# Moving the filter's loads, its folding and its spectrum into the first batch of an attention and long-convolution kernel

## Chip, cores, metric

One core of one Trainium2 chip. The metric is the device time of one execution in microseconds (us), lower is better; a kernel's figure is the median of its runs.

## The reference

Random-feature attention on 8 batches of 8 heads, 576 positions, 64 values per head, then a gated long convolution along the positions:

```python
phi(x)  = concat(cos(x @ omega.T), sin(x @ omega.T)) / sqrt(m)     # m = 128 features
kv      = einsum('bhsm,bhsd->bhmd', phi(k), v);  z = phi(k).sum(axis=2)
attn    = (phi(q) @ kv) / (phi(q) . z)                             # [8, 8, 576, 64] -> x [8, 576, 512]
x1, x2, x3 = split(x @ w_proj, 3)                                  # w_proj [512, 1536]
conv    = irfft(rfft(x2, axis=1) * rfft(filter_fft, axis=0))       # filter_fft [576, 512]
out     = (x1 * conv * x3) @ w_out
```

The FFT is done as matrix products with a cosine/sine basis (`fwd`), over sums and differences of each row with its partner half a period away (the "fold"). The filter needs this once, each batch once.

## The kernel before

A batch goes through four "pairs" (two heads each). The attention of batch b+1 runs between the convolution steps of batch b. Batches 0 and 1 get their k and q transposed by TensorE (`tk`, `tkt`, `tq`), later ones by DMA. The filter was handled like this:

```python
def run(self):
    self.first_loads()                 # k, q, v of batch 0
    self.front(0, 0)                   # features of the first pair
    self.second_loads()                # k, q of batch 1: into yg0, yg1, w
    self.v_loads(1)
    self.weights()                     # basis fwd, filter (into tc0, tc1, yT), w_proj
    for b in range(B + 1):
        for hp in range(4):
            if b < B: self.pair(b, hp)
            if b == hp == 1:
                self.fold_filter()     # six tensor_tensor on VectorE
                self.filter_spectrum() # 17 matmuls, ten copies by ScalarE
            if b: self.hyena(b - 1, hp)      # part 1 is spectrum(b - 1): yp, tc, yg
# ... (cut)
def fold_filter(self):
    with self.tc.issue_after(self.marks["strip", 1, 0].ins):
        for c in range(NC):
            for p, odd, _, n in _filter_rows(c):
                nc.vector.tensor_tensor(ff[c][p:p+n], f[p:p+n, 0], f[p:p+n, 1], SUB if odd else ADD)
# ... (cut)
def k_features(self, b, hp):
    if b < 2: self.first_k(b, hp)      # tk: transpose by TensorE; evacuated by VectorE (b = 0) or ScalarE (b = 1)
    # thk = matmul -> angles by VectorE -> shifted angles by GpSimd -> sine by ScalarE (kf)
# ... (cut)
def spectrum(self, b):                 # of a batch
    for g in range(2):
        # yp = matmuls; tc0, tc1 = yp * filter spectrum (VectorE); yg = tc0 + tc1 (GpSimd)
```

## Time and profile before

| | before |
|---|---|
| median of runs | 424.49 us (423.31 to 424.59, 3 runs; 424.3 beside the changed kernel, with a fourth) |
| span of the profiled run | 419.9 us |
| TensorE, VectorE, ScalarE, GpSimd busy | 80%, 70%, 57%, 53% |
| TensorE's first transposes of batch 1 (`tkt`) | 36.46 us |
| last transposes of batch 0's attention, `tx` | 48.74 us |
| first `tx` of batch 1 | 69.06 us |
| batch 0's spectrum `yp` on TensorE | 79.30 us |

The busy shares are means over very different stages; the marks in the lower half of the table tell more, because each is a point that TensorE, which works in program order, must pass. What fills the SyncE queue early (start, time of issue, what; x is the count):

```profile
11.61 0.64 SPq L319 DMA_DIRECT2D ka<-in_k_dram  x1
...
17.29 8.93 SPq L325 DMA_DIRECT2D qa<-in_q_dram  x2
...
30.96 1.11 SPq L169 DMA_DIRECT2D fwd<-fwdc  x1
32.19 18.52 SPq L200 DMA_DIRECT2D f<-in_moe_filter_fft_dram  x12
```

Batch 1's k and q are issued from 10 to 26 us; only then come the basis (`fwd`) and, to about 50.7 us, the filter `f`. The filter is not needed until 70 us.

### The profile page before, as it was taken

Reading aid. Unit: us, or ns where it says so; the run is one execution under the profiler, and the core shown is the slowest. Engines: PE = TensorE matmul, PEld = TensorE weight load, DVE = VectorE, ACT = ScalarE, POOL = GpSimd, SP = SyncE. Lnnn points to the kernel's source line nnn. Section 1 sums busy time; section 2 is a strip of 40 time slices with the busy share of each in tenths; the row PEclk is TensorE's granted clock in tenths of the full one; section 3 lists DMA queues with packets and bytes.
Section 4 is the critical chain, followed back from the end, with each engine's and each line's share of the span. In section 5 each row is a group of like instructions: output and inputs, shape, how many; then the busy total and the mean of one; then the engine's idle time right before and its main releaser. Section 6 shows DMA issues by size and latency. Waiting matters only on the chain.

```text
span 419.9 us, 9053 instructions
## 1 busy us (share of the span) xinstructions
PE 337.1 (80%) x3714; PEld 225.8 (54%) x3714; DVE 293.4 (70%) x527; ACT 239.8 (57%) x318; POOL 222.1 (53%) x199
## 2 busy tenths in 40 slices
PE   3777666996798977896989889897989788988982
PEld 2565534374455754565556655575556644673650
DVE  3777746679857888497849885788759883862640
ACT  1676764556686458833784488545784478223322
POOL 0546632178653947385836865494726483523350
PEclk9859699799699999999899989996999999999998
DMA  6999999007951592149523873259210012002103
GB/s 175 289 283 270 234 235 156 2 4 152 142 158 32 102 201 82 39 108 156 127 65 101 104 135 114 74 85 172 88 27 0 2 52 64 2 2 70 42 2 113
DMA packets 71465, 44.76 MB, mean 107 GB/s; under 512 B 38656, under 2 KB 64896, under 8 KB 71424
## 3 DMA queue, kind: packets, MB, share of 16 engines
q1 hardware_dynamic: 53712, 34.12, 31.9%
q0 software_dynamic: 17712, 10.06, 17.7%
q8 instruction: 29, 0.48, 0.4%
q14 instruction: 12, 0.10, 0.1%
HBM read 36.83 MB, written 16.52 MB: 127 GB/s over the span
## 4 chain that ended last, share of the span: by engine, by line
PE 36%; DVE 28%; ACT 12%; POOL 11%; issue 8%; DMA 3%; SPq 1%; POOLq 0%; DVEq 0%; ACTq 0%
PE xg L112 10%; DVE tc L557 7%; PE kv L493 6%; PE op L112 5%; ACT qf L477 5%; PE xc L112 4%; DVE angk L418 4%; POOL yT L596 3%; POOL angq L419 3%; DVE angq L418 3%; ACT kf L456 3%; PE nd L510 3%; POOL vl L400 2%; DVE xsd L516 2%; DMA out_dram<-o 2%
## 5 line engine op out<-in xcount | busy, mean ns | idle before, releaser
L477 ACT ACTIVATE qf<-angq 128x1728 f16<-128x1728 int16 (+1 forms) x48 | 70.4, 1480 | 42.6 <-PE nd L510 22.4
L456 ACT ACTIVATE kf<-angk 128x2048 f16<-128x2048 int16 x32 | 61.1, 1909 | 42.0 <-POOL angk L419 31.5
L112 PE MATMUL xg<-xT,wp 128*128 128x288 f16 x512 | 72.0, 286 | 1.1 <-ACT w L574 0.3
L419 POOL TENSOR_SCALAR angk<-angk 128x1024 int32<-128x1024 int32 x32 | 33.5, 1048 | 63.5 <-DVE angk L418 63.1
L418 DVE TENSOR_SCALAR angq<-thq 128x864 int32<-128x864 f32 (+1 forms) x48 | 45.8, 954 | 24.4 <-ACT qf L477 20.0
L112 PEld LDWEIGHTS <-wp 128*128 128x128 f16 x512 | 48.5, 97 | 20.6 <-issue 4.1
L400 POOL TENSOR_TENSOR vl<-vf,vh 128x512 f16<-128x512 f32 x32 | 39.0, 1219 | 28.8 <-ACT vh L399 28.4
L558 POOL TENSOR_TENSOR yg<-tc,tc 128x1024 fp32r<-128x1024 f32 x16 | 37.4, 2358 | 31.5 <-DVE tc L557 30.4
L596 POOL TENSOR_TENSOR yT<-w,cv 128x576 f16<-128x576 f32 x32 | 45.5, 1436 | 15.3 <-DVE cv L595 8.1
L576 DVE TENSOR_TENSOR w<-xg,w 128x288 f32<-128x288 f32 x64 | 27.4, 453 | 37.1 <-ACT w L574 19.6
L419 POOL TENSOR_SCALAR angq<-angq 128x864 int32<-128x864 int32 (+1 forms) x48 | 43.0, 896 | 16.5 <-DVE angq L418 16.1
L493 PEld LDWEIGHTS <-kf 128*128 128x128 f16 x1024 | 43.7, 100 | 13.2 <-issue 11.1
L112 PE MATMUL op<-wo,yT 128*128 128x512 f16 (+1 forms) x160 | 41.4, 390 | 6.0 <-POOL yT L596 6.0
L574 ACT ACTIVATE w<-xg 128x288 f32<-128x288 f32 x64 | 24.6, 407 | 37.7 <-PE xg L112 37.0
L418 DVE TENSOR_SCALAR angk<-thk 128x1024 int32<-128x1024 f32 x32 | 39.0, 1219 | 9.0 <-ACT qf L477 4.4
L510 PE MATMUL nd<-kvz,qf 128*128 128x65 f16 x640 | 27.5, 198 | 20.5 <-DVE kvz L498 19.1
L493 PE MATMUL kv<-vh,kf 128*128 128x65 f16 x512 | 38.5, 198 | 6.1 <-ACT w L574 5.6
L112 PE MATMUL x2p<-wp,eo 128*128 128x512 f16 x160 | 36.3, 379 | 4.9 <-ACT x L546 2.9
L510 PEld LDWEIGHTS <-qf 128*128 128x128 f16 x640 | 25.1, 100 | 26.3 <-issue 23.8
L493 PE MATMUL kv<-vl,kf 128*128 128x64 f16 x512 | 37.3, 197 | 0.8 <-POOL vl L400 0.8
L112 PE MATMUL xc<-inv,yg 128*128 128x288 f32 x128 | 33.4, 352 | 0.1
L609 ACT ACTIVATE o<-op 128x512 f32<-128x512 f32 (+1 forms) x40 | 22.8, 592 | 15.2 <-PE op L112 10.0
(86 smaller groups left out, 628.8 us busy)
## 6 DMA issues: line engine op xcount, KB each, us to landing
vf<-in_v_dram SPq DMA_DIRECT2D x7, 1024.0 KB, 5.3
qD<-in_q_dram POOLq DMA_DIRECT2D x6, 576.0 KB, 7.0
kD<-in_k_dram POOLq DMA_DIRECT2D x6, 512.0 KB, 5.9
ka<-in_k_dram SPq DMA_DIRECT2D x4, 512.0 KB, 10.5
out_dram<-o SPq DMA_DIRECT2D x8, 256.0 KB, 2.6
out_dram<-o SPq DMA_DIRECT2D x8, 224.0 KB
wp<-in_moe_w_proj_dram POOLq DMA_DIRECT2D x1, 1536.0 KB, 16.1
out_dram<-o SPq DMA_DIRECT2D x8, 192.0 KB
```

Source lines behind the costliest of these rows:

```text
L112: nc.tensor.matmul(outap, l, r, start=(i == 0), stop=(i == n - 1))
L400: nc.gpsimd.tensor_tensor(self.vl[hp], vp, vh, ALU.subtract)
L418: self.nc.vector.tensor_scalar(into, th, TO_PHASE, None, ALU.mult)
L419: self.pool_mark = self.nc.gpsimd.tensor_scalar(t[:, 1], t[:, 0], 1.0, TURN / 4, ALU.mult, ALU.add)
L456: self.marks["k", b, hp] = nc.scalar.activation(kf.rearrange("p t r a c m -> p t (r a c m)"), ang, AF.Sin, scale=TO_ANGLE)
L477: nc.scalar.activation(self.qf[b][:, :, a0 : a0 + n].rearrange("p t a r i -> p t (a r i)"), ang, AF.Sin, scale=TO_ANGLE)
L493: nc.tensor.matmul(ps[:, hh, t, : 1 + D] if i < 5 else ps[:, hh, t, :D], l, r_, start=(i == 0), stop=(i == len(terms) - 1),)
L510: nc.tensor.matmul(ps[:, c], qfh[:, t, SOFF[c] : SOFF[c] + 128], kvz[:, hh, t], start=(t == 0), stop=(t == 1),)
L557: nc.vector.tensor_tensor(t[i], ps[:, None, :].broadcast_to([128, 2, DM]), hc, ALU.mult)
L558: nc.gpsimd.tensor_tensor(self.yg[g], t[0], t[1], ALU.add)
L576: nc.vector.tensor_tensor(w[:, ns], ps, w[:, ns], ALU.mult)
L596: nc.gpsimd.tensor_tensor(self.yT[b][:, dc], self.w.pop((b, dc)).rearrange("p a s -> p (a s)"), cv.rearrange("p c z i -> p (c z i)"), ALU. ...
```

## The change

The intent: the filter's fold and spectrum stand in series for nine microseconds, once per run, so do them earlier, where engines idle. The basis and the filter are loaded directly behind batch 0, in front of batch 1; GpSimd folds; the spectrum and the first transposes of batch 1 go between the pairs of batch 0.

```diff
 def run(self):
         self.front(0, 0)
-        self.second_loads()
-        self.v_loads(1)
         self.weights()
+        self.second_loads()              # v of batch 1 now inside, behind the first k and q blocks
@@
-                if b == hp == 1:
-                    self.fold_filter()
-                    self.filter_spectrum()
+                if b == 0:
+                    self.opening(hp)
+    def opening(self, hp):
+        if hp == 1:
+            self.fold_filter()
+            self.first_k_tails(1)
+            self.first_k(1, 0)
+        elif hp == 2:
+            self.filter_spectrum(0)
+            self.first_k(1, 1)
+        elif hp == 3:
+            self.filter_spectrum(1)
+            self.filter_spectrum(2)
@@ fold_filter: no issue_after any more
-                    nc.vector.tensor_tensor(...)
+                nc.gpsimd.tensor_tensor(...)
@@ buffers of the loads
-        f{c}: tc0, tc1, tc1, tc0, yT                 ka1: yg0, yg1      qa1: w (4 tiles)
+        f0, f1, f4: yg0, yg1, yT; f2, f3 as halves in w (17 DMAs, 12 before)
+        ka1: tc0 (2 tiles)   qa1: tc1 (2 tiles)
@@ filter_spectrum: hre, him become one tile h; one copy fewer per group
... (cut)
```

More of the change, by code (lines that the diff above doesn't have):

```diff
@@ L39 @@
 QW = 4 * S
-FTAG = [("tc0", 2), ("tc1", 2), ("tc1", 2), ("tc0", 2), ("yT", 1)]
 QGROUPS = [(0, 3, 3), (6, 3, 3), (12, 2, 2)]
@@ L194, in filter_loads @@
         every4 = self.filt.rearrange("(z i r) d -> r i z d", z=2, r=4)
+        whole = {0: ("yg0", 1), 1: ("yg1", 1), 4: ("yT", 1)}
         self.fl = []
         for c in range(NC):
-            f = mo.tile([128, 2, DM], FP32, name=f"f{c}", tag=FTAG[c][0], bufs=FTAG[c][1])
+            if c in whole:
+                tag, bufs = whole[c]
+                f = mo.tile([128, 2, DM], FP32, name=f"f{c}", tag=tag, bufs=bufs)
+                parts = [(f, slice(0, 2))]
+                self.fl.append([f[:, 0], f[:, 1]])
+            else:
+                halves = [mo.tile([128, 1, DM], FP32, name=f"f{c}_{z}", tag="w", bufs=4) for z in range(2)]
+                parts = [(f, slice(z, z + 1)) for z, f in enumerate(halves)]
+                self.fl.append([f[:, 0] for f in halves])
             for p, _, lo, n in _filter_rows(c):
                 for blk, i, m, at in _pieces(lo, n, EB):
-                    nc.sync.dma_start(f[p + at : p + at + m], every4[BLOCKS[blk], i : i + m])
-            self.fl.append(f)
+                    for f, z in parts:
+                        nc.sync.dma_start(f[p + at : p + at + m], every4[BLOCKS[blk], i : i + m, z])
     def fold_filter(self):
@@ L207, in fold_filter @@
         self.ff = ff = [ffs[c // 2][:, c % 2] for c in range(NC)]
-        with self.tc.issue_after(self.marks["strip", 1, 0].ins):
-            nc.vector.memset(ff[2], 0.0)
-            for c in range(NC):
-                f = self.fl[c]
-                for p, odd, _, n in _filter_rows(c):
-                    nc.vector.tensor_tensor(
-                        ff[c][p : p + n], f[p : p + n, 0], f[p : p + n, 1], ALU.subtract if odd else ALU.add
-                    )
-    def filter_spectrum(self):
-        nc, cst, fwd, ff = self.nc, self.cst, self.fwd, self.ff
-        self.hre = [cst.tile([128, 2, DM], FP16, name=f"hre{g}", tag=f"hre{g}") for g in range(2)]
-        self.him = [cst.tile([128, 2, DM], FP16, name=f"him{g}", tag=f"him{g}") for g in range(2)]
-        self.hmix = cst.tile([128, DM], FP16, name="hmix", tag="hmix")
-        hre, him = self.hre, self.him
-        for g in range(2):
-            ps = self.bank([128, DM], f"hps{g}")
-            _mm_acc(nc, ps, [(fwd[:, 2 * g, c], ff[c]) for c in GRP[2 * g]])
-            nc.scalar.copy(hre[g][:, 0], ps)
-            nc.scalar.copy(him[g][:, 1], ps)
-            ps = self.bank([128, DM], f"hpi{g}")
-            _mm_acc(nc, ps, [(fwd[:, 2 * g + 1, c], ff[c]) for c in GRP[2 * g + 1]])
-            nc.scalar.copy(hre[g][:, 1], ps)
-            nc.scalar.mul(him[g][:, 0], ps, -1.0)
-            if g == 0:
-                nc.scalar.copy(him[0][:1, 1], ps[:1])
-                nc.vector.memset(hre[0][:1, 1], 0.0)
-                nc.vector.memset(him[0][:1, 0], 0.0)
-        ps = self.bank([128, DM], "hpm")
-        _mm_acc(nc, ps, [(fwd[:, 5, c], ff[c]) for c in GRP[5]])
-        nc.scalar.copy(self.hmix, ps)
@@ new lines, in fold_filter, with filter_spectrum @@
+        nc.gpsimd.memset(ff[2], 0.0)
+        for c in range(NC):
+            f = self.fl[c]
+            for p, odd, _, n in _filter_rows(c):
+                nc.gpsimd.tensor_tensor(
+                    ff[c][p : p + n], f[0][p : p + n], f[1][p : p + n], ALU.subtract if odd else ALU.add
+                )
+    def filter_spectrum(self, g):
+        nc, cst, fwd, ff = self.nc, self.cst, self.fwd, self.ff
+        if g == 2:
+            self.hmix = cst.tile([128, DM], FP16, name="hmix", tag="hmix")
+            ps = self.bank([128, DM], "hpm")
+            _mm_acc(nc, ps, [(fwd[:, 5, c], ff[c]) for c in GRP[5]])
+            nc.scalar.copy(self.hmix, ps)
+            return
+        h = self.h[g] = cst.tile([128, 4, DM], FP16, name=f"h{g}", tag=f"h{g}")
+        ps = self.bank([128, DM], f"hps{g}")
+        _mm_acc(nc, ps, [(fwd[:, 2 * g, c], ff[c]) for c in GRP[2 * g]])
+        nc.scalar.copy(h[:, 0::3], ps[:, None, :].broadcast_to([128, 2, DM]))
+        ps = self.bank([128, DM], f"hpi{g}")
+        _mm_acc(nc, ps, [(fwd[:, 2 * g + 1, c], ff[c]) for c in GRP[2 * g + 1]])
+        nc.scalar.copy(h[:, 1], ps)
+        nc.scalar.mul(h[:, 2], ps, -1.0)
+        if g == 0:
+            nc.scalar.copy(h[:1, 3], ps[:1])
+            nc.gpsimd.memset(h[:1, 1:3], 0.0)
@@ L310, in second_loads @@
         qta = mo.tile([128, 4 * D], FP32, name="qta1", tag="osb", bufs=2)
-        ka = [mo.tile([128, 4, 4 * D], FP32, name=f"ka1_{i}", tag=f"yg{i}") for i in range(2)]
-        qa = [mo.tile([128, 2, 4 * D], FP32, name=f"qa1_{i}", tag="w", bufs=4) for i in range(4)]
+        ka = [mo.tile([128, 4, 4 * D], FP32, name=f"ka1_{i}", tag="tc0", bufs=2) for i in range(2)]
+        qa = [mo.tile([128, 4, 4 * D], FP32, name=f"qa1_{i}", tag="tc1", bufs=2) for i in range(2)]
         self.first[1] = (
             ktl.rearrange("p j d -> p (j d)"), qta,
-            [ka[h // 4][:, h % 4] for h in range(H)], [qa[h // 2][:, h % 2] for h in range(H)],
+            [ka[h // 4][:, h % 4] for h in range(H)], [qa[h // 4][:, h % 4] for h in range(H)],
             self.ident32, FP32,
@@ L320, in second_loads @@
         nc.sync.dma_start(qta, self.q[1, :, 512:, :].rearrange("h (i r) d -> h i (r d)", r=4))
-        for i in range(2):
-            nc.sync.dma_start(qa[i], self.fours(self.q, 1, 2 * i, 2))
+        nc.sync.dma_start(qa[0], self.fours(self.q, 1, 0, 4))
+        self.v_loads(1)
         nc.sync.dma_start(ka[1], self.fours(self.k, 1, 4, 4))
-        for i in range(2, 4):
-            nc.sync.dma_start(qa[i], self.fours(self.q, 1, 2 * i, 2))
+        nc.sync.dma_start(qa[1], self.fours(self.q, 1, 4, 4))
     def turned_loads(self, b):
@@ L424, in k_tail_features @@
         self.kft[b] = self.ft.tile([128, 2, 4, 128], FP16, name=f"kft{b}", tag="kft")
-        if b < 2:
+        if b == 0:
             self.first_k_tails(b)
@@ L442, in k_features @@
         blocks = slice(4 * hp, 4 * hp + 4)
-        if b < 2:
+        if b == 0 or b == 1 and hp > 1:
             self.first_k(b, hp)
@@ L553, in spectrum @@
             t = [mo.tile([128, 2, DM], FP32, name=f"tc{b}_{g}_{i}", tag=f"tc{i}", bufs=2) for i in range(2)]
-            for i, hc in ((0, self.hre[g]), (1, self.him[g])):
+            for i, hc in ((0, self.h[g][:, :2]), (1, self.h[g][:, 2:])):
                 ps = self.bank([128, DM], f"yp{b}_{g}_{i}")
@@ L614, in run @@
         for name in ("vf", "kT", "qT", "kf", "kft", "qf", "kvz", "xsd", "xT", "w", "yT", "marks", "pool_marks",
-                     "first"):
+                     "first", "h"):
             setattr(self, name, {})
@@ L621, in run @@
         self.front(0, 0)
+        self.weights()
         self.second_loads()
-        self.v_loads(1)
-        self.weights()
         self.v_split_tails(0)
@@ L629, in run @@
                     self.pair(b, hp)
-                if b == hp == 1:
-                    self.fold_filter()
-                    self.filter_spectrum()
+                if b == 0:
+                    self.opening(hp)
                 if b:
                     self.hyena(b - 1, hp)
+    def opening(self, hp):
[9 more added lines that the diff above has]
+            self.filter_spectrum(2)
     def pair(self, b, hp):
```

## The prediction

> **What bounds the kernel now.** I began with busy time by stretch, to see which part of the run the change can reach; it edits only what is issued before batch 1 is through. Columns: stretch, its length, then busy time of TensorE, its weight loads, VectorE, ScalarE and GpSimd, the granted clock, the DMA share and GB/s.
>
> ```profile
> 0.00:50.00 50.00, 30.90 (x379) 24.12 (x380) 33.79 (x70) 27.89 (x26) 24.03 (x31) 0.81 1.02 251
> 50.00:70.00 20.00, 14.35 (x193) 10.16 (x191) 9.68 (x18) 12.23 (x17) 4.97 (x5) 0.96 1.12 205
> 70.00:79.50 9.50, 6.76 (x18) 2.40 (x19) 5.96 (x11) 6.25 (x11) 1.12 (x1) 0.64 0.28 62
> 79.50:100.00 20.50, 19.35 (x226) 13.72 (x224) 16.43 (x26) 12.19 (x18) 12.47 (x11) 1.00 0.20 55
> ```
>
> Up to 70 us no engine is full (TensorE 62% to 72%, VectorE 48% to 68%), yet the DMA share is above 1: the opening is a chain of short steps fed by saturated transfers. From 79.5 us TensorE is 94% busy. Between them lies a hole of 9.5 us in which GpSimd works 1.1 us and DMA little. The chain that ended last shows it (start, duration, what):
>
> ```profile
> 70.02 0.07 DVE xsd L516
> 70.08 0.42 issue
> 70.50 0.27 DVE ff L209
> ...
> 71.23 2.21 DVE ff L213 x2
> ...
> 73.48 0.69 DVE ff L213
> ...
> 74.21 0.59 PE hps L112
> ...
> 77.78 1.68 PE hpm L112 x5
> 79.46 1.94 PE yp L112 x9
> ```
>
> VectorE folds the filter, then 17 matmuls make its spectrum, and batch 0's spectrum `yp` waits for both: 79.46 - 70.08 = 9.4 us in series, once per run. That is what the change goes after.
>
> Next I looked at what fills the DMA engines early. From 18 to 28 us it is the cast load of `w_proj` on the software queue. A sample from 20 to 22 us (queue: packets, MB, share of 16 engines):
>
> ```profile
> q0 software_dynamic: 113, 0.35, 87.2%
> q1 hardware_dynamic: 114, 0.11, 20.4%
> ```
>
> One packet of each queue in turn; the software packet costs 0.872 x 16 x 2 us / 113 = 247 ns, the hardware one 57 ns. So the hardware queue, which carries everything the change reorders, is held to 55 GB/s. Between 28 and 33 us, alone, it makes 358 GB/s. Last, when batch 1's first blocks are used (TensorE in order of time):
>
> ```profile
> 30.26 0.72 PE L529 MATMUL tx<-ident,xsd 128*128 128x128 f16 x5
> 30.78 0.75 PE L352 MATMUL tk<-ident,ka 128*128 128x128 f32 x4
> ...
> 36.46 0.39 PE L352 MATMUL tkt<-ident,ktl 128*128 128x128 f32 x2
> 36.89 0.63 PE L352 MATMUL tk<-ident,ka 128*128 128x128 f32 x4
> ```
>
> The `tk` at 30.78 belongs to batch 0 (its last pair); `tkt` and `tk` at 36.5 are batch 1's. The semaphore records show batch 1's first k block had landed by 22.1 us, fourteen before its use.
>
> **What the Trainium skill says.** "DMA: Bandwidth & Descriptors", section "Queues, rings and completion order": each DMA engine round-robins between its queue rows by packet. The 113 against 114 packets agree. "GPSIMD Engine Reference", section "4.1 Engine selection": two-input elementwise work is about 2x slower on GpSimd than on VectorE. Here a 128x512 subtraction of the same types (`vl`) takes 1.12 us in most cases and VectorE's fold 0.68 us at the median: 1.6x. "SBUF — State Buffer", section "SBUF: two separate sides": VectorE and GpSimd share a port pair under an exclusive lock. The trace fits: two casts `vth` normally of about 0.3 us take 4.26 us at 101.36, while GpSimd has no gap. In the opening VectorE mostly reads PSUM, so I charge nothing for the folds there. "Perfetto Trace Analysis", section "Optimization Strategy", recommends interleaving regimes with different limits: the idea of this change.
>
> **The change part by part.**
>
> *Removed from the path.* The fold and spectrum at 70 to 79.5 us: -9.4 us. Six folds leave VectorE for GpSimd, 6 x 1.12 = 6.7 us; GpSimd is idle for about half of 20 to 40 us.
>
> *Moved in the SP queue.* Batch 1's loads now come after the basis (0.98 MB) and the filter (each of 576 rows is loaded with its partner, 2.36 MB). At the same time the instruction order of the changed kernel puts batch 1's `tkt` and first `tk` on TensorE before batch 0's last `tk`, so at 30.8 us instead of 36.5. Needed earlier, loaded later. When does the block land? Batch 0's loads land at 17.3 us as now, and by 18 us the queue will have moved half the basis (it moves 0.49 MB of batch 1 by then now). What each of 16 engines must still do, with packet times from the trace's packet records: basis 4 x 0.403 = 1.6 us; filter 1152 packets of 2 KB, 72 x 0.100 = 7.2; rest of `w_proj` 525/16 x 0.247 = 8.1; k tails 32 x 0.018 = 0.6; the block 32 x 0.05 = 1.6. Sum 19.1 us, so 37.1 us, about 38 with completion. An estimate, and the floor if 17 smaller filter DMAs issue without gaps. TensorE stands in order behind it: batch 0's last `tk` moves from 30.8 to about 38.5: **+7.7 us**. GpSimd also waits for the first filter block (landing near 26.7 us) before `vl` of pair 1, now at 25.4, +2.5 us, but this ends before the longer wait and is inside it. The other folds lie under it too.
>
> *Added in pairs 2 and 3 of batch 0.* ScalarE gets the spectrum's copies, two of 128x1024 (estimate 1.1 us each) and about six at a pitch of 0.48 us, 5.1 us in all. It idles 20 - 7.43 - 6.25 = 6.3 us between 40 and 60 us, but those gaps are waits for angles, and the copies stand in order in front of batch 1's features and of the transposes' evacuations, whose banks TensorE then needs. TensorE gets 17 matmuls at 0.43 us, 7.3 us, where it idles 4.5 + 1.9 us. I take **+2.5 us** (0 to 5).
>
> *A new buffer wait.* Half of batch 1's k block now sits in the `tc0` ring until pair 3 of batch 1, after batch 0's spectrum. The instruction order shows the third `tc` product waiting for GpSimd's `yg`, which it doesn't now. `yg` takes 2.36 us; now the third product starts at 82.42 with the second still draining; 0.68 us of it is filled with `ymix`, put first: **+1.9 us**, once.
>
> *Noise of order.* Merging the filter's two tiles into one saves a copy; steady batches keep their instructions. Spectra start 45 us apart later on (132.8, 177.8, 223.1), and nothing there changes.
>
> Sum: -9.4 + 7.7 + 2.5 + 1.9 = +2.7 us, 427.2 from 424.5; I say 427.
>
> **Rivals.** *The load wait is short.* If the block lands by 32 us, the opening costs 3 to 4 us and the total is about 422. For: the wait rests on one landing time, and large basis packets take a larger turn against `w_proj` than 1 KB packets do. Against: all those bytes must still pass before the block, and the engines are full. *The lost time is absorbed.* The 52.5 us from batch 0's spectrum to batch 1's is 7 longer than later intervals, with the 4.26 us casts in it; another phase between GpSimd and VectorE could avoid them, giving 418 to 421. Against: the order there is unchanged, and with it probably the clash. *ScalarE becomes the bound of the opening*, its in-order copies pushing batch 1's first features by more than 5 us, and late q blocks starve behind the 6.9 KB packets of `inv`: 431 to 434. For: hand-laying the copies gave me up to 5 us.
>
> **Range and chances.** The gain of 9.4 us is sure within 1 us. The wait is 3 to 10, the crowding 0 to 5, the buffer wait 1 to 2.5, and a shift of phase is worth up to 4 either way. This gives 418 to 434 for 8 in 10. Faster by over 2% means below 416.0: the wait nearly gone and no crowding, 0.11. Slower by over 2% means above 433.0: 0.14. The rest 0.75.
>
> **What would show it.** Right: TensorE idle for 4 us or more, ended by the DMA of `ka` or `ktl`, between 31 and 40 us; batch 0's last `tk` near 38.5; no `ff` on VectorE, and `yp` directly behind batch 1's first `tx`, at about 82 to 83 us instead of 79.5; GpSimd's folds between 26 and 38; a gap of 2 us in the `tc` products of batch 0. Wrong: the k block landing before 33 us, `yp` before 77, or a different length of the stretch from 100 us to the end by more than 4 us, which I don't predict.

## The result, and the profile after

428.87 us (426.84 to 430.0, 4 runs) against 424.3 us of the kernel before in the same call. Ratios here are computed as the mean time of one kernel's fast runs over that of the other's fast runs of the same rounds, so they are not quite the ratio of the medians quoted: 1.0107, 95% interval 1.0064 to 1.0149. By the 2% line that is "the same"; by the interval it is slower by 0.6% to 1.5%.

Busy time by stretch of the changed kernel, columns as in the prediction's first view:

```profile
0.00:50.00 50.00, 25.68 (x290) 20.16 (x291) 24.64 (x53) 18.86 (x16) 21.92 (x26) 0.76 0.91 245
50.00:70.00 20.00, 13.56 (x182) 8.76 (x180) 12.95 (x23) 17.62 (x23) 12.19 (x15) 0.91 1.18 222
70.00:79.50 9.50, 7.97 (x61) 4.69 (x61) 3.76 (x7) 7.24 (x12) 2.88 (x3) 1.00 0.28 60
79.50:100.00 20.50, 17.25 (x215) 11.60 (x212) 14.77 (x25) 9.55 (x13) 10.88 (x9) 1.00 0.03 5
```

TensorE lost 5.2 us of work in the first stretch (25.68 against 30.90), ScalarE went from 12.23 to 17.62 us in the second, and from 70 to 79.5 us TensorE now does 61 matmuls instead of 18, at a granted clock of 1.00 instead of 0.64. VectorE has 288.4 us of work in all instead of 293.4, GpSimd 231.0 instead of 222.1. The chain that ended last:

```profile
15.77 16.65 DMA f<-in_moe_filter_fft_dram
...
35.56 5.87 DMA ka<-in_k_dram
...
41.57 1.94 PE tk L356 x8
...
51.44 0.90 ACT h L236
...
82.74 0.28 PE tx L533 x5
83.02 2.59 PE yp L111 x12
```

The opening's chain now runs through the filter's DMA, then the DMA of batch 1's first k block, then TensorE, then a ScalarE copy of the filter's spectrum (`h`); at 83 us `yp` follows `tx` with nothing between. The two waits on TensorE:

```profile
39.81 0.66 PE L356 MATMUL tkt<-ident,ktl 128*128 128x128 f32 x2 [4.91 <-DMA ktl<-in_k_dram]
41.57 1.94 PE L356 MATMUL tk<-ident,ka 128*128 128x128 f32 x8 [1.10 <-DMA ka<-in_k_dram]
```

The eight `tk` are four of batch 1 and then the four of batch 0's last pair, which so begin at about 42.4 us instead of 30.78 (in the records the fifth of the eight starts at 42.45). The queue that issues the loads:

```profile
11.55 22.58 SPq L209 DMA_DIRECT2D f<-in_moe_filter_fft_dram  x17
...
35.56 0.53 SPq L324 DMA_DIRECT2D ka<-in_k_dram  x1
```

The 17 filter DMAs keep the queue for 22.6 us; the first k block is issued at 35.56 and lands 5.9 us later. Last, the four products of batch 0's spectrum on VectorE, before and then after:

```profile
80.15 1.23 DVE L557 TENSOR_TENSOR tc<-yp,hre 128x1024 f32<-128x1024 f32 x1 [2.87 <-PE yp L112]
...
83.55 1.22 DVE L557 TENSOR_TENSOR tc<-yp,him 128x1024 f32<-128x1024 f32 x1
```

```profile
83.93 2.35 DVE L561 TENSOR_TENSOR tc<-yp,h 128x1024 f32<-128x1024 f32 x2
...
88.77 2.36 DVE L561 TENSOR_TENSOR tc<-yp,h 128x1024 f32<-128x1024 f32 x2 [1.35 <-POOL yg L562]
```

Before, the last of the four began 3.4 us after the first; after, the third waits for GpSimd's `yg`. First start to last end is 4.6 us before (80.15 to 84.77) and 7.2 us after (83.93 to 91.13).

The marks, in one table (us; "last `tx`" is batch 0's fourth):

| run | `tkt` | last `tx` | `tx` of batch 1 | `yp` | median of runs |
|---|---|---|---|---|---|
| before | 36.46 | 48.74 | 69.06 | 79.30 | 424.3 |
| after | 39.81 | 60.07 | 82.58 | 82.85 | 428.87 |
| turns late | 42.36 | 60.70 | 83.73 | 84.01 | 427.52 |
| w_proj late | 43.30 | 64.27 | 87.75 | 88.02 | 431.88 |
| spectrum back | 38.41 | 57.48 | 75.49 | 80.51 | 427.07 |
| own buffers | 39.67 | 60.23 | 83.95 | 84.23 | 425.9 |
| before + fold on GpSimd | 36.42 | 48.71 | 70.00 | 75.08 | 419.03 |
| the same + half the spectrum early | 36.00 | 48.28 | 70.26 | 72.92 | 417.35 |
| before + early transposes | 30.07 | 46.40 | 65.35 | 75.01 | 418.29 |
| whole filter tiles | 39.75 | 60.15 | 83.88 | 84.15 | 429.8 |
| loads and fold alone | 39.61 | 56.79 | 76.23 | 81.25 | 428.95 |
| k block first | 30.77 | 60.86 | 81.03 | 81.31 | 425.02 |
| combined | 30.61 | 47.19 | 65.86 | 68.52 | 411.39 |
| 69 rows | 43.23 | 64.22 | 87.62 | 87.89 | 432.05 |

The kernel before ran beside each group of runs at 422.9 to 424.3 us. The marks come from one profiled run each, which in kernels with the same early loads differ by up to 1.4 us (`tkt` at 39.81, 38.41 and 39.67 in "after", "spectrum back" and "own buffers").

### The profile page after: what moved, and what is told of

Same layout as the page of the kernel before. It is cut to its first block, busy times and chain, and to the rows that moved or that the text cites. A ratio compares the mean times of both kernels' runs of the same rounds, so it can differ in the third digit from the quotient of the medians.

```text
span 425.1 us, 9051 instructions
## 1 busy us (share of the span) xinstructions
PE 337.7 (79%) x3714; PEld 226.5 (53%) x3714; DVE 288.4 (68%) x518; ACT 239.6 (56%) x316; POOL 231.0 (54%) x207
## 4 chain that ended last, share of the span: by engine, by line
PE 34%; DVE 22%; ACT 15%; DMA 10%; POOL 8%; issue 7%; SPq 2%; POOLq 0%; ACTq 0%; DVEq 0%
PE xg L111 9%; DVE tc L561 7%; ACT qf L481 6%; PE op L111 6%; PE xc L111 5%; PE kv L497 5%; DMA f<-in_moe_filter_fft_dram 4%; ACT kf L460 3%; DVE angk L422 3%; POOL yT L600 3%; DMA out_dram<-o 3%; POOL angq L423 3%; PE nd L514 3%; DVE xsd L520 2%; DMA qa<-in_q_dram 2%
## 5 line engine op out<-in xcount | busy, mean ns | idle before, releaser
L561 DVE TENSOR_TENSOR tc<-yp,h 128x1024 f32<-128x1024 f32 x32 | 37.0, 1215 | 1.5 <-POOL yg L562 1.3
L514 PEld LDWEIGHTS <-qf 128*128 128x128 f16 x640 | 24.1, 98 | 24.3 <-issue 18.6
L111 PE MATMUL xc<-inv,yg 128*128 128x288 f32 x128 | 34.6, 363 | 0.1
```

Of the source, the lines that this page charges most:

```text
L111: nc.tensor.matmul(outap, l, r, start=(i == 0), stop=(i == n - 1))
L514: nc.tensor.matmul(ps[:, c], qfh[:, t, SOFF[c] : SOFF[c] + 128], kvz[:, hh, t], start=(t == 0), stop=(t == 1),)
L561: nc.vector.tensor_tensor(t[i], ps[:, None, :].broadcast_to([128, 2, DM]), hc, ALU.mult)
```

## The experiments

My theory after the result was: the first k block of batch 1 lands late because it stands behind the filter, TensorE waits for it in order, and this eats the gain; the crowding and the buffer wait are smaller. The diffs are shortened to the lines that carry the change.

**Early transposes undone.** Batch 1's transposes at the places of before, all else as changed:

```diff
-        if b == 0 or b == 1 and hp > 1:
+        if b < 2:
             self.first_k(b, hp)
@@ opening
-            self.first_k_tails(1)
-            self.first_k(1, 0)
```

> Theory A (TensorE stands in order behind batch 1's first k block, placed before batch 0's last pair): with the transposes of batch 1 back at their old places and the loads as in the changed kernel, batch 0's last k transposes start near 35 us instead of 42, the block lands at 41 as before and nobody waits for it more than 1 us; 428.9 falls by 5 to 8 us, to 421 to 424. Rival B (the loads themselves bound the opening, wherever the transposes stand): the wait only moves behind pair 2 or to the q and v blocks of batch 1, and the time stays at 427 to 429.

Measured: 427.52 us (424.9 to 430.72), ratio to before 1.0105 (1.0064 to 1.0146): nothing came back. Batch 0's last `tk` is at 35.43, as expected, though still 4.65 us later than in the kernel before; and time is lost again 10 us later. On TensorE:

```profile
47.29 0.39 PE L435 MATMUL tht<-om,kT 64*128 64x128 f16 x4 [4.54 <-ACT kT L363]
```

The wait is now for ScalarE's evacuation of `tkt`, which stands in order behind the copies of the filter's first spectrum (43.50 to 46.88). At batch 0's last `tx` TensorE waits another 5.42 us, for VectorE's `xsd`, with VectorE at work almost without a gap from 52.66 to 60.2 us. The wait had moved to ScalarE and VectorE, so putting TensorE's order right was not enough.

**w_proj later.** Its cast load issued behind pair 2's angles, so that the filter has the engines to itself:

```diff
-        with self.tc.issue_after(self.pool_marks["k", 0, 0].ins):
+            with self.tc.issue_after(self.pool_marks["k", 0, 2].ins):     # now inside opening(1)
                 self.in_weights()
```

> The cast load of w_proj is issued after the angles of pair 2 instead of pair 0, so it no longer shares the DMA engines with the basis and the filter. Theory A with the packet round robin as cause of the late landing: the first filter block lands near 21 us instead of 28, batch 1's k block before 32 instead of 41.4, TensorE's wait falls under 1 us, and the time to 418 to 422. Rival C (the 17 small filter DMAs with at most 8 under way set the landing, not w_proj): the block still lands after 36 us and the time falls by less than 4 us. Rival D (w_proj then starves batch 1's v and q blocks): the wait moves there, 424 to 428.

Measured: 431.88 us (429.04 to 433.37), ratio 1.0199 (1.0163 to 1.0235): slower. The first fold came at 25.76 instead of 28.13, but `tkt` waited 14.6 us for its DMA, until 43.3. From 30 to 42 us `w_proj` took 70.5% of the engines' time. In both kernels what shares the engines with `w_proj` moves slowly (0.11 MB in 2 us in the prediction's sample; the k tails, issued from 28.95 us, here); the move only changed what that is.

**Spectrum back.** The filter's spectrum behind pair 1 of batch 1 again, loads, folds and transposes as changed:

```diff
         elif hp == 2:
-            self.filter_spectrum(0)
             self.first_k(1, 1)
... (cut: the two calls at hp == 3 go as well)
@@ run
+                if b == hp == 1:
+                    for g in range(3):
+                        self.filter_spectrum(g)
```

> Loads, folds on GpSimd and early transposes as in the changed kernel, but the filter's spectrum (17 matmuls and 8 copies) back behind pair 1 of batch 1. My working of the prediction (crowding in the opening costs 2.5 us, the place behind pair 1 costs 5 us or more of matmuls in series): 2 to 5 us slower than the changed kernel, 431 to 434. Rival (the copies in front of batch 1's evacuations cost as much as they save): within 1 us of the changed kernel; if ScalarE's crowding is worse than that, faster.

Measured: 427.07 us (425.83 to 428.96), ratio 1.0092 (1.0062 to 1.0123): no slower than the whole change. On TensorE:

```profile
75.49 0.44 PE L533 MATMUL tx<-ident,xsd 128*128 128x128 f16 x5
...
80.51 1.71 PE L111 MATMUL yp<-x,fwd 128*128 128x512 f16 x6 [0.18 <-ACT h L242]
```

With the folds gone, the spectrum costs only 80.51 - 75.76 = 4.75 us in series. More than the folds' own time is saved: in the kernel before, the last 13 of the 17 matmuls started 0.43 us apart (74.21 to 79.30, granted clock 0.54 there), here they start 0.215 us apart (granted clock 1.00), which for 13 is an estimated 2.3 us less. Why the clock was low there, just after TensorE's waits for the folds, no run shows. And batch 1's first `tx` is 7.1 us earlier than in the changed kernel, 1.4 of it because the loads happened to land sooner (`tkt` 38.41 against 39.81). So the spectrum placed between the pairs cost about 5.7 us there, and saved 4.75. (The same difference of two single profiles with the transposes late, "turns late" less "loads and fold alone" below, is 7.5 us.)

**Own buffers.** Batch 1's second k and q blocks out of the rings of `tc`:

```diff
-        ka = [mo.tile(..., tag="tc0", bufs=2) for i in range(2)]
+        ka = [mo.tile(..., tag="tc0", bufs=2), mo.tile(..., tag="yT")]
+        qa0 = mo.tile(..., tag="tc1", bufs=2); qa1 = two halves, tag="w"
```

> The second halves of batch 1's k and q go to buffers that are free by then instead of the ring of the spectrum's products, the rest as in the changed kernel. If the third product's wait for GpSimd's sum is on the path: the four products of batch 0 follow each other in 4.6 us instead of 7.2 and the time falls by 1.5 to 3 us, to 426 to 427.5. If it is hidden by other waits: no change, 428 to 429.

Measured: 425.9 us (424.4 to 427.94), ratio 1.0064 (1.003 to 1.0097), 0.43% or 1.8 us below the changed kernel's 1.0107, though with overlapping intervals. It was run at another time. The four products take 4.61 us again instead of 7.2. So the buffer wait is real, 2.6 us in the trace; that the time gains the predicted size fits, but is not clear of noise.

So far every part that I took back returned little. The next four runs turn the question round: which part of the change gains if done alone on the kernel before, and is it the count of DMAs that makes the loads late?

**Fold alone.** The kernel before, folds on GpSimd behind its last angles of pair 1 of batch 1:

```diff
-        with self.tc.issue_after(self.marks["strip", 1, 0].ins):
-                    nc.vector.tensor_tensor(...)
+        with self.tc.issue_after(self.pool_mark.ins):        # called behind pair (1, 0)
+                    nc.gpsimd.tensor_tensor(...)
```

> The kernel before with one part of the change alone: the six folds go from VectorE to GpSimd, issued behind GpSimd's last angles of pair 1 of batch 1 (59.1 us before), where GpSimd then idles 8.2 us (60.0 to 68.2). Loads, transposes and the place of the spectrum stay as before. Theory (the fold in series was worth about 4 us, the loads and crowding are what cost): six folds of 1.26 us end at about 67.6, the spectrum starts directly behind batch 1's first tx at 69.3 and takes about 4.75 us as in the run with the spectrum put back, so yp starts near 74.2 instead of 79.5 and the time falls by 4 to 5 us, to about 419.5 (ratio 0.989). Rival 1 (what is gained is lost in later clashes of GpSimd and VectorE or in waiting for the phase of the next batch): yp at 74 but time within 1.5 us of before. Rival 2 (the filter has not landed by 60, or the folds push the angles of pair 2 of batch 1): GpSimd waits for the DMA of f, angles later than 69.5, less than 2 us gained.

Measured: 419.03 us (418.49 to 419.97), ratio 0.9908 (0.9884 to 0.9932). GpSimd in order of time:

```profile
61.39 7.62 POOL L213 TENSOR_TENSOR ff<-f 128x512 f16<-128x512 f32 x6
69.15 1.04 POOL L419 TENSOR_SCALAR angk<-angk 128x1024 int32<-128x1024 int32 x1
```

Six folds of 1.27 us fit GpSimd's idle 8.19 us almost exactly. The angles that follow start at 69.15 us instead of 68.20, and batch 1's `tx` at 70.00 instead of 69.06; `yp` follows at 75.08. The wait for VectorE's `ff` is gone, without moving any load.

**Fold and half of the spectrum.** In addition the first six matmuls and four copies in front of ScalarE's features of pair 2 of batch 1. (The spectrum also gets its one tile `h` here, with two copies fewer; in series that is worth little, 4.80 us in "fold alone" against 4.75 with `h` in "spectrum back".)

```diff
         ang = self.turns(th, f"k{b}_{hp}")
+        if b == 1 and hp == 2:
+            self.filter_spectrum(0)                          # 1 and 2 stay behind pair (1, 1)
```

> As the run before it, and the first half of the spectrum (6 matmuls, 4 copies by ScalarE, 2.7 us) goes in front of ScalarE's features of pair 2 of batch 1, where ScalarE idled 3.0 us (66.2 to 69.3 before) and TensorE about 1 us. Theory: these copies are hidden in that gap, the rest of the spectrum behind tx takes about 2.7 us, yp near 72.5, another 1 to 2 us gained on the run before it (about 418). Rival (the copies push the features, the transposes' place and with them everything behind by as much as they save): tx_0 of batch 1 at 70.5 or later and the time the same as the run before it within 1 us.

Measured: 417.35 us (415.86 to 418.74), ratio 0.9863 (0.9833 to 0.9892); `tx` of batch 1 at 70.26, `yp` at 72.92. The copies, put where ScalarE idled 3.0 us, moved `tx` by 0.26 us and brought `yp` forward by 2.16; the same copies between the pairs of batch 0 were not so nearly free.

**Early transposes alone.** The kernel before with batch 1's first transposes where the change has them:

```diff
+                if b == 0 and hp == 1:
+                    self.first_k_tails(1); self.first_k(1, 0)
+                if b == 0 and hp == 2:
+                    self.first_k(1, 1)
```

> The kernel before with another part of the change alone: the transposes of batch 1's k tails and of its first two k blocks move to where the change has them (between the pairs of batch 0); loads, fold and spectrum as before. The first block had landed by 22.1 us there, so no wait for a DMA is expected at 31 to 33 us. Theory (early transposes are worth nothing or little in themselves, and cost only through the late landing): tkt and tk near 31 to 32 without a DMA wait, within 1.5 us of before (ratio 0.997 to 1.003). Rival (they crowd TensorE and ScalarE between the pairs by themselves): last pair of batch 0 later by 2 us or more and the time up by 2 us or more.

Measured: 418.29 us (417.36 to 419.73), ratio 0.9891 (0.9864 to 0.9917). Both my theory (no effect) and its rival (slower) were wrong: this part gains 1.1% by itself. On TensorE:

```profile
30.07 0.39 PE L352 MATMUL tkt<-ident,ktl 128*128 128x128 f32 x2
30.43 1.06 PE L352 MATMUL tk<-ident,ka 128*128 128x128 f32 x8
...
46.40 0.50 PE L529 MATMUL tx<-ident,xsd 128*128 128x128 f16 x5 [1.27 <-DVE xsd L516]
```

No DMA wait, the last `tx` of batch 0 at 46.40 instead of 48.74, and `tx` of batch 1 at 65.35 instead of 69.06, 3.7 us sooner. With the k blocks transposed early, the features of batch 1 reach ScalarE with shorter waits: its sines for the first q group of batch 1 start at 45.94 instead of 47.87, and those for the second k block at 50.80 instead of 55.51, after a wait for GpSimd's angles of 0.30 instead of 3.23 us.

**Whole filter tiles.** The changed kernel with filter blocks 2 and 3 whole, in the buffers of `x2` and `eo`:

```diff
-        whole = {0: ("yg0", 1), 1: ("yg1", 1), 4: ("yT", 1)}
+        whole = {0: ("yg0", 1), 1: ("yg1", 1), 2: ("x2", 1), 3: ("eo", 1), 4: ("yT", 1)}
```

> The changed kernel with filter blocks 2 and 3 loaded whole (row and partner in one DMA, as before the change) into two buffers that are first used later, instead of in halves: 11 DMAs for the filter instead of 17, the same bytes. Theory (the filter's issue, 22.6 us for 17 DMAs, each waiting for one about 8 before it, held the queue below its rate): the filter is issued 5 to 8 us sooner, ktl's issue moves from 34.2 to 27 to 29, tkt and tk of batch 1 start 3 to 6 us earlier (34 to 37), total down 2 to 4 us against the changed kernel. Rival (bytes and w_proj's packets set the landing, not the count of DMAs): tkt and tk within 1.5 us of 39.8 and 41.6, total within 1 us of the changed kernel.

Measured: 429.8 us (428.64 to 432.37), ratio 1.0166 (1.0135 to 1.0197), not better. (It made 12 DMAs, not the 11 that I had counted.) The k tails were issued at 31.41 instead of 34.17 and the block at 32.98 instead of 35.56, yet `tkt` began at 39.75 against 39.81 and `tk` at 41.64 against 41.57. The theory that issuing held the loads back falls. Transfers from 28 to 34 us, the changed kernel and then this one (packets, MB; share of 16 engines):

```profile
DMA packets 545, 0.90 MB, mean 150 GB/s; under 512 B 108, under 2 KB 108, under 8 KB 545
q1 hardware_dynamic: 540, 0.89, 63.9%
```

```profile
DMA packets 745, 1.11 MB, mean 185 GB/s; under 512 B 220, under 2 KB 220, under 8 KB 745
q1 hardware_dynamic: 742, 1.11, 84.5%
```

Nearly all of it is the filter, and it moves 150 and 185 GB/s, where batch 1's blocks in the kernel before made 358 alone. On the average some 10 and 13.5 of the 16 engines are at work. The last run told of, below, asks why.

Two runs then put the parts together and two parts apart.

**Combined.** Loads of before, early transposes, folds on GpSimd, half of the spectrum early (the three gains above, no other edit):

```diff
+                if b == 0 and hp == 1:
+                    self.first_k_tails(1); self.first_k(1, 0)
+                if b == 0 and hp == 2:
+                    self.first_k(1, 1)
+                if b == 1 and hp == 0:
+                    self.fold_filter()                       # GpSimd
+ front(1, 2): self.filter_spectrum(0);  behind pair (1, 1): (1), (2)
```

> The parts of the change that gained alone, put together on the loads of before: early transposes of batch 1 (alone 0.9891), folds on GpSimd behind its angles of pair 1 of batch 1 and the first half of the spectrum in ScalarE's gap (together 0.9863). Theory (each part shortens another stretch of the opening; what spoils the change is the order of its loads): the gains add, ratio 0.974 to 0.979, about 412 to 414 us, tx_0 of batch 1 near 66, yp near 69, faster than both kernels. Rival (with the earlier transposes GpSimd reaches the folds at about 56 us, before the filter has landed, and the wait shifts to it): GpSimd waits for the DMA of f by more than 2 us, angles of pair 2 of batch 1 later than 66.5, ratio 0.983 or worse.

Measured: 411.39 us (411.21 to 411.8, 5 runs), ratio 0.9717 (0.9688 to 0.9746). It beats both kernels, by 2.8% and, over the two ratios, by 3.9%. GpSimd's folds and TensorE:

```profile
56.57 7.62 POOL L213 TENSOR_TENSOR ff<-f 128x512 f16<-128x512 f32 x6
```

```profile
65.86 0.44 PE L529 MATMUL tx<-ident,xsd 128*128 128x128 f16 x5
...
68.52 2.84 PE L112 MATMUL yp<-x,fwd 128*128 128x512 f16 x12
```

The folds start at 56.57 without a wait for the filter, and `yp` starts 10.8 us sooner than before. The two gains alone would have given 1.1% + 1.4% = 2.5%; they add, and the little more lies within the intervals.

**Loads and fold alone.** The change without early transposes and with the spectrum behind pair 1 of batch 1, that is, "turns late" and "spectrum back" in one:

```diff
     def opening(self, hp):
         if hp == 1:
             self.fold_filter()
-            self.first_k_tails(1) ...                        # and all else of opening
```

> The changed kernel with its order of loads and its early folds on GpSimd alone: batch 1's transposes at the places of before, the whole spectrum behind pair 1 of batch 1. The run with the folds on GpSimd and the loads as before gave 419.0 us (0.9908); this one differs from it in the order of loads and the time of the folds. Theory (the order of the loads is what costs, through k, q and v of batch 1 landing late and the folds delaying the low parts of v): TensorE waits for a DMA or for what follows from one between 36 and 46 us, last pair of batch 0 ends 4 us or more later than in that run, 424 to 428 us. Rival (the crowding by the spectrum is what costs, the order of loads hardly): within 2 us of 419.

Measured: 428.95 us (426.12 to 429.95), ratio 1.0121 (1.0088 to 1.0153), 9.9 us above "fold alone" (2.1% over the two ratios), from which it differs in the order and buffers of the loads and in the time of the folds. It was run at another time. Batch 0's last `tx` is at 56.79, 8.1 us later; TensorE waited 3.93 us for ScalarE's evacuation of `tkt` and 4.21 us for VectorE's `xsd`. For a DMA of batch 1 TensorE waited only 0.31 us. Earlier, GpSimd waited for the filter, and TensorE for GpSimd:

```profile
27.00 1.26 POOL L220 TENSOR_TENSOR ff<-f 128x512 f16<-128x512 f32 x1 [2.88 <-DMA f<-in_moe_filter_fft_dram]
```

```profile
29.39 0.37 PE L497 MATMUL kv<-vl,kf 128*128 128x64 f16 x4 [3.88 <-POOL vl L404]
```

In the kernel before that last wait is 0.77 us. Batch 0's last `tk` comes at 33.51 instead of 30.78, before any load of batch 1 is needed, so the early folds are part of the cost. No run has the new order of loads with the folds late, so the two are not told apart. Together they are what costs, and by more than the crowding, which adds 60.70 - 56.79 = 3.9 us to this mark ("turns late" less this run).

**k block first.** The changed kernel, the k tails and the first k block of batch 1 in front of basis and filter:

```diff
+        self.early_k()          # ktl1 in "ymix", ka1_0 in "x2" (free until batch 0's projection)
         self.weights()
         self.second_loads()
```

> The changed kernel with the k tails and the first k block of batch 1 (0.63 MB) loaded in front of the basis and the filter, the block in a buffer that is free until the projection of batch 0; everything else as the change has it (GpSimd's folds end up somewhat later in its order). Theory (the +11.6 us at batch 0's last k transposes is the late landing of this block): tkt and tk start at 30 to 33 us without a wait for their DMA, the last tx of batch 0 moves from 60.1 to 53 to 56, and 3 to 6 us come back: 423 to 426 us. Rival (something else in the opening takes over: q and v of batch 1 still land late, or the folds hold GpSimd): tkt and tk at 30 to 33 but the last tx of batch 0 still after 58, less than 2 us gained on the changed kernel.

Measured: 425.02 us (421.28 to 425.86), ratio 1.0027 (0.9991 to 1.0062), 0.8% or some 3.4 us better than the changed kernel. The time agrees with the theory, the trace half with the rival: `tkt` at 30.77 without a wait, but batch 0's last `tx` at 60.86. What took over, on GpSimd and then on ScalarE:

```profile
32.51 1.26 POOL L220 TENSOR_TENSOR ff<-f 128x512 f16<-128x512 f32 x1 [5.09 <-DMA f<-in_moe_filter_fft_dram]
```

```profile
34.81 1.91 ACT L465 ACTIVATE kf<-angk 128x2048 f16<-128x2048 int16 x1 [5.72 <-POOL angk L428]
```

GpSimd waits 5.09 us for the first filter block (0.63 MB more stand in front of it), holding the angles behind the fold, and so ScalarE's features. In the changed kernel this wait lay inside the longer one. In every run here that loads and folds the filter this early, some engine waits for it or for what it holds up.

**69 rows.** The run with whole tiles, and one 72-row piece of the filter cut unevenly:

```diff
+                cuts = ((0, 69), (69, 3)) if c == 4 and m == 72 else ((0, m),)
```

> The changed kernel with whole filter tiles as in the run with 12 filter DMAs, and the last piece of the filter, 72 rows, cut into 69 and 3 rows (13 DMAs, the same bytes). The first k block landed no sooner there although it was issued 2.6 us sooner, and between 28 and 34 us only about 10 (17 DMAs) or 13 (12 DMAs) of 16 engines were at work in the samples. Theory (the spread decides: the Trainium skill, DMA: Bandwidth & Descriptors, section Why a DMA increments its semaphore by 16 and not by 1, says a DMA is spread over the largest number of engines up to 16 that divides its outer dimension, the lowest-numbered ones, so 72, 56 and 40 rows take 12, 14 and 10 engines and load the first engines more than the last): 69 rows go to 3 engines, 23 rows each instead of 6, with the 3 rows 24: 36 packets of 2 KB more on each of these, at 96 to 150 ns (both seen) 3.5 to 5.4 us, and the k tails and the k block behind them land later by that: tkt from 39.75 to 43 to 45, tk from 41.6 to 45 to 47, and the time rises by 2 to 5 us over that run. Rival (bytes alone set the landing): tkt and tk within 1 us of 39.75 and 41.6, time within 1.5 us.

Measured: 432.05 us (430.22 to 433.12), ratio 1.0206 (1.0153 to 1.0259), about 0.4% (1.7 us) above the run with whole tiles, less than the 2 to 5 us expected and with overlapping intervals, so the trace has to decide. On TensorE:

```profile
43.23 0.66 PE L360 MATMUL tkt<-ident,ktl 128*128 128x128 f32 x2 [8.81 <-DMA ktl<-in_k_dram]
```

`tkt` is 3.5 us later (43.23 against 39.75) and `tk` 3.2 us (44.84 against 41.64), a little under my 45 to 47. By the packet records the filter's last packet ends at 41.7 us instead of 37.9. The bytes were the same, and the k tails were issued at 33.21 us, between the times of the two other runs (31.41 and 34.17). So how rows spread over engines moves the landing. The Trainium skill gives the rule ("DMA: Bandwidth & Descriptors", section "Why a DMA increments its semaphore by 16 and not by 1"): a DMA takes the largest number of engines, up to 16, that divides its outer dimension on both sides, and the lowest-numbered ones. The packet counts of the whole runs agree. Here are the hardware queue's packets, MB and share in the changed kernel, with whole tiles, and with 69 rows:

```profile
q1 hardware_dynamic: 53750, 34.12, 30.9%
```

```profile
q1 hardware_dynamic: 53680, 34.12, 31.0%
```

```profile
q1 hardware_dynamic: 53674, 34.12, 30.4%
```

The data packets are the same in all three; what differs is the number of 4-byte packets (2294, 2224 and 2218 in the records). If each engine that a DMA uses adds one of them, the rule gives 16 + 16 + 10 + 12 + 16 = 70 fewer without the five halves, and 12 - 3 - 3 = 6 fewer with 69 + 3 rows. Both are met exactly; with all 16 engines for every DMA it would be 80 fewer and 16 more.

All twelve runs of experiments gave the right result.

## Why the prediction was right or wrong

The result lies in the range, in the class given 0.75, and 1.9 us above the predicted time. Step by step, with the sum of the prediction beside what the marks show:

| step | predicted | measured in before and after |
|---|---|---|
| batch 0's last `tk` behind batch 1's first | +7.7 | +11.6 (30.78 to 42.4) |
| crowding in pairs 2 and 3 | +2.5 | +1.9 (first `tx` of batch 1 +13.5, less 11.6) |
| fold and spectrum in series | -9.4 | -10.0 (`yp` +3.6 in the chain, less 13.5) |
| buffer wait of the third `tc` | +1.9 | +2.6 |
| sum | +2.7 | +6.1; +5.8 at batch 1's `yp` (131.60 to 137.39), +5.2 in the spans, +4.6 in the medians |

**Gain in series: right.** `yp` follows `tx` directly, at 83.02 us in the chain (predicted 82 to 83), and no `ff` is on VectorE. The runs add that a good part of this gain did not need the move: the fold alone, done by GpSimd in its own hole, takes 4.2 us off `yp` and 0.9% off the time.

**The wait for the k block: mechanism right, term too small.** TensorE idled 4.91 us for `ktl` and 1.10 for `ka`, in the window I named, but the block landed near 41.4, not 38. The failed step is "filter 1152 packets of 2 KB, 72 x 0.100 = 7.2", which deals the packets evenly to 16 engines. The filter's pieces have 72, 56, 40, 32 and 16 rows; by the skill's rule they take 12, 14, 10, 16 and 16 engines, which puts 46 rows, 92 packets, on the first engines instead of 72. At the 96 to 150 ns per packet that the records show, the extra 20 make an estimate of 1.9 to 3.0 us of the 3.4 missed. The packets were also slower than assumed, 116 ns on average over the 1152 instead of 100, and so the term would have been 92 x 0.116 = 10.7 instead of 7.2, 3.5 more (an estimate that leaves the other terms as they were). The filter's last packet ended at 38.1 us, where the sum's first three terms give 34.9; from there to the landing the sum held. The 69-row run shows that the spread moves the landing; the whole-tile run shows that "17 smaller filter DMAs issue without gaps", my own caveat, was not the cause. Why packets take 96 ns in one stretch and about 150 in another stays open.

**The crowding: right by luck.** The 1.9 us in the table is a difference of two things of which the prediction knew one. "Early transposes" gained 3.7 us on the mark `tx` of batch 1 when the loads were in time, and "spectrum back" shows the spectrum's copies and matmuls costing about 5.7. If the two add, which no run tests, 5.7 - 3.7 = 2.0, close to the 1.9 measured. The prediction sized the crowding at 2.5 (range to 5) and gave the early transposes nothing but a penalty; by these figures both were wrong, and the errors cancelled. "ScalarE becomes the bound of the opening" was the rival that named more than 5, though its total of 431 to 434 did not come: TensorE waited for ScalarE's `h` copies (1.85 us at 54.89, 1.40 at 67.11), and ScalarE was busy 17.62 of 20 us.

**The buffer wait: right.** The third product waits for `yg`, and the four products take 2.6 us longer, 0.7 more than predicted; with own buffers that goes, and 1.8 us come back in the ratios, within noise.

**GpSimd's own wait: hidden, as said, and then not.** The first fold came at 28.13 instead of 26.7 us. TensorE waited 5.26 us for the `vl` behind it, but then still 4.91 us for the k tails, so this cost nothing more; each of the six took 1.26 us instead of the 1.12 assumed; with the k block first it was laid bare and cost 5.09 us of GpSimd's time.

**Later stretches: right.** From 100 us to the end nothing changed in kind; the pair of casts that takes 4.26 us before takes 4.25 after, 5.1 us later. The rival that a new phase would avoid them did not come true in any run, the combined one included (4.26 us at 90.56).

Where the expected gain went: into the new order of the loads and the early folds that come with it ("loads and fold alone" is 2.1% slower than "fold alone"), which no run parts, and for a smaller part into the spectrum's place, which costs about what it saves. The parts, with the loads left as they were and the folds and the spectrum put into gaps just in front of their use, gain 2.8%.

## What to carry to other kernels

When work is pulled forward into a hole, look first for a hole that needs no load to move; here GpSimd's idle 8 us just in front of the use was enough, and the same folds 30 us earlier, with the order of loads that this needs, cost more than they freed. Test each part of a compound change alone on the kernel before: two parts gained 1% each inside a package that lost 1%. And when estimating when a load lands, count packets on the busiest engine, not the average, and look for row counts that divide by 16 (which the rule suggests; the run here only made the spread worse).

## What the Trainium skill lacked or had wrong

- "DMA: Bandwidth & Descriptors": its rule for the spread over engines held (70 and 6 packets fewer, as it gives; 69 + 3 rows instead of 72 put `tkt` 3.5 us later); I had not applied it when I predicted. What it lacks is what a train of unevenly spread DMAs does to the loads behind it: 0.90 MB in 6 us (150 GB/s at 63.9% of the engines) and, with 12 DMAs, 1.11 MB (185 GB/s at 84.5%), and the block behind landing at the same time in both.
- The same page's round robin by packet held (127 against 125 packets from 36 to 38 us in "w_proj late"), and the cost of it for small packets beside large ones is worth a warning there: with `w_proj` moved behind the filter, k tails of small packets were waited for 14.6 us.
- "Perfetto Trace Analysis": the advice to interleave stages with different limits lacks the caution that the inserted work stands in program order in front of what follows on the same engine; the spectrum's copies and matmuls cost about 5.7 us in one place, and half of them moved `tx` by 0.26 us in a gap of ScalarE's elsewhere.
- "SBUF — State Buffer" names the lock that VectorE and GpSimd share. Every kernel profiled here shows the casts of batch 2's v tails at 4.25 to 4.27 us for two (one of them alone takes about 3.93 of it), and at 0.28 to 0.38 us each in later batches; that the lock is the cause fits, but no run here shows it, so this point stays open.
